# Fewer, larger loads between the two layers of a cached decode step on one core

## The chip, the cores and the metric

The kernel runs on one core of one Trainium2 chip. Its engines here are TensorE (PE, with its weight loads as PEld), VectorE (DVE), ScalarE (ACT), GpSimd (POOL) and SyncE (SP), and SP issues the transfers, which the core's 16 DMA engines carry out. The metric is the device time of one execution in microseconds (us), the median of several runs. One further execution is profiled, and every time of a stage below is from it.

## The reference

Two equal layers run over four tokens (B = 4) of width D = 512. Each layer is attention over a cache, then a gated feed-forward:

```
x = x + A(layernorm(x))      # q = x@wq (32 heads of 128); per kv head g of 8: scores q.k over 4096 positions,
                             # softmax, times v; concat @ wo
x = x + B(layernorm(x))      # silu(x@w1) * (x@w3), width 1792, then @ w2
# the same A and B, with the same cache and weights, once more
```

All is float32. Both layers read the whole K and V cache (each 4 x 8 x 4096 x 128, 64 MiB), so almost all of the time's work is the reading of some 298 MB, while the arithmetic has only 16 rows per kv head.

## The kernel before, in words

**Memory.** One large tile, `arena`, of 218 units (a unit is 256 floats, 1 KB, in each of 128 partitions, so 128 KB in all) holds everything that is loaded. Units 0 to 63 are for wq, 64 to 127 for wo, 128 to 191 for what is kept between layers (V of kv head 7, `TURN`), and units 192 to 215 are a **ring** that the feed-forward's weights pass through, together with the four units at `WO` (64 to 67). Units 214 and 215 of the ring are, until the last attention step of layer 0, part of the turned probabilities `pT`.

**Order.** The list `plan` is written at build time: every load, with the units where it goes, or none (then the first free place that is large enough is taken). `pump` issues loads from it strictly in order, all from SP, as long as the next one's units have been given back. `done` and `vacate` give units back when the work that reads them has been written, and in the running program SP waits there for that work's semaphore. So a load that has to wait holds up all later ones. Completion counters of the loads are eight in number and are taken in turn, so a load also waits until the eighth load before it has landed.

**Layer 0.** Per kv head: `scores` (PE, from K), softmax pieces on DVE and ACT, `weigh` (PE, from V). K and V of a head come as loads of 64 units (8 MB).

**Between the layers.** After the last `weigh`, the kernel runs `busy(14)` (matmuls without use that fill PE's time), `project_o` for the eight heads from wo, `collect` (the sum over heads, and the residual and norm's first part), and `feed_forward`: products with w1's and w3's first 256 columns of each quarter (`w1a`, `w3a`: four pieces each of 4 units, one per 128 rows of D), then the remaining 192 columns (`w1b`, `w3b`: four pieces of 3 units), and w2 (`down`, seven pieces of 4 units). Then `project_q` of layer 1 and the first K, whose first half comes as seven pieces called `half` through the same ring. Each product starts as soon as its piece has landed, and gives its units back when its matmuls are done. For wo, `project_o(g)` reads 8 units per head, in order of g; in the kernel before, wo comes in five loads of 32, 16, 8, 4 and 4 units, so heads 0 to 3 wait for the first alone.

**Layer 1** runs the heads in reverse order, and its last feed-forward uses larger pieces already.

The lines that the prediction speaks of: `project_o`'s matmuls (L497 for heads 0 to 6, L490 for head 7, which also is `down`), the filling matmuls of `busy` (L293) and `idle` (L299), `collect` (L336, L339), the feed-forward's products (L530), and SP's issues (L183).

Of the kernel before, what the change touches and what calls it, by code (L numbers as in the profile page):

```python
# [30 lines left out]
KB = 256  # L31
ARENA = 218
TURN = HKV - 1
SPLIT = 4
# [4 lines left out]
def tile_decode_layers(ctx: ExitStack, tc: tile.TileContext, x, kt, v, wq, wo, w1, w3, w2, w2s, out):  # L39
    nc = tc.nc  # L40
# [8 lines left out]
    WQ, WO, KEPT = 0, 64, 128  # L49
# [6 lines left out]
    def take(n, at=None):  # L56
        if at is not None and at < WO:
            return at
        for i, (lo, size) in enumerate(free):
            if at is None and state["next"] > ring["to"]:  # L60

                end = min(lo + size, PT)
                if lo < WO + 4 and end > WO:
                    if WO - lo >= n:
                        end = WO
                    else:
                        lo = WO + 4
                if end - lo < n:
                    continue
                a = lo  # L70
                lo, size = free[i]
            else:
                a = lo if at is None else at
            if lo <= a and a + n <= lo + size:
                free[i:i + 1] = [(p, s) for p, s in ((lo, a - lo), (a + n, lo + size - a - n)) if s]
                return a
        return None
# [10 lines left out]
    def load(src, per, keys, at=None):  # L88
        plan.append((src, per, keys, at))

    def cache(which, layer, g, parts, skip=0):
        src = (kt if which == "k" else v)[g]
        r = 8 * skip
        for n in parts:
            at = KEPT + r if (which, layer, g) in (("v", 0, TURN), ("k", 1, TURN - 2)) else None
            load(src[:, r * KB:(r + n) * KB], 8, [(which, layer, g, r // 8 + j) for j in range(n // 8)], at)
            r += n

    def weights(name, src, layer, parts, per, at=None, first=0):
        r = 0  # L100
        for n in parts:
            load(src[:, r * KB:(r + n) * KB], per, [(name, layer, first + r // per + j) for j in range(n // per)],
                 None if at is None else at + r)
            r += n

    order = [list(range(HKV)), list(reversed(range(HKV)))]
# [5 lines left out]
        else:  # L112
            cache("v", 0, n - 1, (64,))
    cache("v", 0, TURN, (32, 32))
    weights("wo", wo, 0, (32, 16, 8, 4, 4), 4, WO)

    def piece(name, i, at):

        w, layer, lo, n, per = {"w1a": (w1, 0, 4 * i, 4, 4), "w3a": (w3, 0, 4 * i, 4, 4),
                                "w1b": (w1, 0, 16 + 3 * i, 3, 3), "w3b": (w3, 0, 16 + 3 * i, 3, 3),  # L120
                                "w2": (w2, 0, 4 * i, 4, 2), "half": (kt[TURN], 1, 4 * i, 4, 4)}[name]
        weights(name, w[:, lo * KB:(lo + n) * KB], layer, (n,), per, at, 2 * i if name == "w2" else i)

    RING = KEPT + 64
    slots = [WO] + [RING + 4 * i for i in (5, 4, 3, 2, 1, 0)]
    for i in range(4):
        piece("w1a", i, (slots[6], slots[1], slots[2], slots[3])[i])
    for i in range(4):
        piece("w3a", i, (slots[4], slots[5], slots[0], slots[6])[i])
    for i in range(4):  # L130
        piece("w1b", i, RING + 21 - 3 * i)
    for i in range(2):
        piece("w3b", i, RING + 9 - 3 * i)
    piece("w2", 0, slots[0])
    for i in range(2, 4):
        piece("w3b", i, RING + 9 - 3 * i)
    for i in range(1, 7):
        piece("w2", i, slots[i])
    for i in range(7):
        piece("half", i + 1, slots[i])  # L140
    ring["to"] = len(plan) - 1
    cache("k", 1, TURN, (8, 8, 16), SPLIT)
    for n in range(1, HKV):
        cache("k", 1, order[1][n], {1: (8, 8, 8, 8, 16, 16), 2: (32, 32)}.get(n, (64,)))
        if n > 1:
            cache("v", 1, order[1][n - 1], (32, 32) if n == HKV - 1 else (64,))
    cache("v", 1, 0, (32, 16, 16))
# [16 lines left out]
    def pump():  # L164
        while state["next"] < len(plan):
            src, per, keys, at = plan[state["next"]]
            n = src.shape[-1] // KB
            if isinstance(per, slice):

                if keys not in where:  # L170
                    a = take(n)
                    if a is None:
                        return
                    where[keys] = a
                    nc.gpsimd.memset(arena[:, a * KB:(a + n) * KB], 0.0)
                a = where[keys]
                nc.sync.dma_start(arena[per, a * KB:(a + n) * KB], src)  # L177
                state["next"] += 1
                continue
            a = take(n, at)  # L180
            if a is None:
                return
            nc.sync.dma_start(arena[:, a * KB:(a + n) * KB], src)  # L183
            i = state["next"]
            if i == 0:
                nc.sync.dma_start(xt[:8], x[:8])
            left[i] = (len(keys), a, n)
            for j, key in enumerate(keys):
                where[key] = (a + j * per, per, i)
            state["next"] += 1  # L190
# [5 lines left out]
    def done(*key):  # L196
        i = where[key][2]
        k, a, n = left[i]
        left[i] = (k - 1, a, n)
        if k == 1:  # L200
            give(a, n)
            pump()

    def vacate(*key):
        a, n, _ = where[key]
        give(a, n)
        pump()

    xt = const.tile([P, KC, B], F32, name="xt")
    nc.scalar.dma_start(xt[8:], x[8:])  # L210
    pump()

    ident = const.tile([P, P], F32, name="ident")
    make_identity(nc, ident)
    few = const.tile([P, 4], F32, name="few")
    one, half, spare, unit = (few[:, i:i + 1] for i in range(4))
# [495 lines left out]
```

## Time and profile before

| what | before |
|---|---|
| median of 3 runs | 704.77 us (704.68 to 704.85) |
| profiled execution | 704.5 us |
| its span | 702.7 us, so 1.8 us lie around it |
| HBM read | 298.33 MB, mean 425 GB/s over the span |
| PE busy | 402.9 us (57%) |
| DVE, ACT, POOL busy | 85.2, 38.0, 7.0 us |
| loads and stores | 96 |

The span begins with the first instruction of the program and ends with the last. A PE row of the timeline gives start, length, line, output and inputs, count, and in brackets the idle time before it and what ended that. "x8" in the trace counts passes: a float32 matmul appears there twice.

### The profile page before, as it was taken

To read this page: it belongs to the slowest core of one execution; us is meant where nothing else is said; L and a number is where in the kernel's file an instruction comes from. 1 tells how busy PE (TensorE), PEld (TensorE's weight loads), DVE (VectorE), ACT (ScalarE), POOL (GpSimd) and SP (SyncE) were. 2 spreads that over 40 slices of the span, in tenths; PEclk is the share of its full clock that TensorE was granted. 3 is DMA by queue.
4 is the path that set the end of the run, shared out by engine and by line. 5 is a ranking of instruction groups with operands and counts; after the bars stand their busy time and mean duration, and the time that the engine had idled before them with its cause. 6 is when DMAs were issued, how large, how long until landed. Compare 5 with 4: busy or idle time off the path is not lost. (4 is left out here: it accounts for less than half of the span.)

```text
span 702.7 us, 7079 instructions
## 1 busy us (share of the span) xinstructions
PE 402.9 (57%) x3172; PEld 135.5 (19%) x3172; DVE 85.2 (12%) x291; ACT 38.0 (5%) x87; POOL 7.0 (1%) x12
## 2 busy tenths in 40 slices
PE   2555453555555454447888884365564545467677
PEld 1112011111111111112233321011120111122234
DVE  2001010101001010101111111020010101010111
ACT  0000000000000000102001000000000000000100
POOL 0000000000000000000000000000000000001000
PEclk9986787767778777779999997588787878788899
DMA  9999999999999999999999999999999999999997
GB/s 418 429 407 466 422 422 422 451 426 425 430 451 422 429 430 444 425 421 427 415 405 408 416 437 441 448 425 419 452 433 425 422 451 426 433 419 432 420 426 287
DMA packets 13174, 298.85 MB, mean 425 GB/s; under 512 B 1608, under 2 KB 1736, under 8 KB 6216
## 3 DMA queue, kind: packets, MB, share of 16 engines
q1 hardware_dynamic: 13008, 298.39, 99.2%
q8 instruction: 25, 0.41, 0.2%
q14 instruction: 6, 0.04, 0.0%
q10 hardware_dynamic: 135, 0.01, 0.0%
HBM read 298.33 MB, written 0.07 MB: 425 GB/s over the span
## 5 line engine op out<-in xcount | busy, mean ns | idle before, releaser
L462 PE MATMUL o_ps<-arena 128*32 128x512 f32 x1024 | 143.1, 706 | 149.6 <-DMA arena<-in_v 137.7
L415 PE MATMUL s_ps<-arena,qpad 128*32 128x512 f32 x1020 | 147.5, 732 | 92.0 <-DMA arena<-in_kt 92.0
L462 PEld LDWEIGHTS o_ps<-arena 128*32 128x32 f32 x1024 | 37.0, 127 | 253.3 <-issue 224.3
L415 PEld LDWEIGHTS s_ps<-arena,qpad 128*32 128x32 f32 x1020 | 39.3, 131 | 183.9 <-issue 176.4
L471 DVE SCALAR_TENSOR_TENSOR p<-o_ps,parts,p 128x512 f32<-128x512 f32 x16 | 12.0, 751 | 267.4 <-PE o_ps L462 267.4
L425 DVE TENSOR_REDUCE top<-s_ps 128x1 f32<-128x512 f32 x16 | 11.1, 691 | 196.6 <-PE s_ps L415 196.6
L469 ACT ACTIVATE p<-o_ps,parts 128x512 f32<-128x512 f32 x16 | 11.0, 687 | 188.5 <-PE o_ps L462 182.3
L293 PE MATMUL m_ps<-ident,rows 128*32 128x256 f32 (+1 forms) x84 | 20.9, 352 | 0.0
L353 PE MATMUL o_ps<-arena,xpad 128*32 128x512 f32 x112 | 15.5, 676 | 7.8 <-DMA arena<-in_wq 7.8
L448 PE MATMUL t_ps<-ident,p 128*128 128x128 f32 x64 | 10.9, 295 | 13.5 <-ACT p L442 13.5
L475 PE MATMUL t_ps<-ident,p 128*128 128x128 f32 x64 | 10.5, 287 | 13.9 <-DVE p L471 13.8
L435 ACT ACTIVATE f<-d 128x1 f32<-128x1 f32 x16 | 3.2, 203 | 251.0 <-DVE d L433 251.0
L497 PE MATMUL x_ps<-arena,qT 128*4 128x512 f32 x112 | 13.8, 592 | 5.1 <-DVE qT L483 3.6
L442 ACT ACTIVATE p<-s_ps,top 128x512 f32<-128x512 f32 x16 | 10.9, 684 | 75.9 <-PE t_ps L475 75.9
L449 DVE COPY arena<-t_ps 128x512 f32<-128x512 f32 x16 | 11.1, 691 | 9.3 <-PE t_ps L448 9.3
L475 PEld LDWEIGHTS t_ps<-ident,p 128*128 128x128 f32 x64 | 6.7, 140 | 28.0 <-DVE p L471 28.0
L448 PEld LDWEIGHTS t_ps<-ident,p 128*128 128x128 f32 x64 | 7.0, 145 | 22.2 <-ACT p L442 19.2
L293 PEld LDWEIGHTS m_ps<-ident,rows 128*32 128x32 f32 x84 | 9.0, 110 | 9.0 <-issue 3.5
L530 PE MATMUL s_ps<-arena,xpad 128*32 128x192 f32 (+1 forms) x128 | 7.9, 359 | 1.5 <-DMA arena<-in_w 1.5
L530 PE MATMUL o_ps<-arena,xpad 128*32 128x192 f32 (+1 forms) x128 | 8.1, 359 | 1.0 <-DMA arena<-in_w 0.9
L490 PE MATMUL x_ps<-arena,qT 128*4 128x256 f32 x88 | 6.6, 379 | 2.4 <-DMA arena<-in_w 1.7
L353 PEld LDWEIGHTS o_ps<-arena,xpad 128*32 128x32 f32 x112 | 3.5, 121 | 17.2 <-DMA arena<-in_wq 8.7
(108 smaller groups left out, 147.6 us busy)
## 6 DMA issues: line engine op xcount, KB each, us to landing
arena<-in_v SPq DMA_DIRECT2D x5, 4096.0 KB, 38.4
arena<-in_w SPq DMA_DIRECT2D x17, 512.0 KB, 9.3
arena<-in_kt SPq DMA_DIRECT2D x2, 4096.0 KB, 18.7
arena<-in_wq SPq DMA_DIRECT2D x1, 7168.0 KB
arena<-in_kt SPq DMA_DIRECT2D x6, 1024.0 KB, 11.2
arena<-in_kt SPq DMA_DIRECT2D x3, 2048.0 KB, 16.7
arena<-in_wo SPq DMA_DIRECT2D x1, 4096.0 KB, 24.0
arena<-in_v SPq DMA_DIRECT2D x2, 2048.0 KB, 36.9
```

The source lines that it names most:

```text
L293: nc.tensor.matmul(m_ps[0:32, (4 - w) * P:], rows, ident.unsqueeze(1).broadcast_to([P, w, P]), start=True, stop=True)
L353: nc.tensor.matmul(ps[32 * k:32 * k + 32, :], xpad[:, 32 * k + lo:32 * k + lo + 32], w[:, k, :], start=first, stop=last)
L415: nc.tensor.matmul(s_ps[32 * b:32 * b + 32, :], qpad[:, 32 * b + lo:32 * b + lo + 32], k[:, j, :], start=(blk == 0), stop=(blk == NB - 1))
L425: nc.vector.tensor_reduce(top[:, 0:1], s_ps, axis=AX.X, op=ALU.max, negate=True)
L448: nc.tensor.transpose(t_ps[:, i, :], p[:, i * P:(i + 1) * P], ident)
L449: nc.vector.tensor_copy(pT.rearrange("p i r -> p (i r)"), t_ps.rearrange("p i r -> p (i r)"))
L462: nc.tensor.matmul(o_ps[32 * b:32 * b + 32, :], pT[:, i, 32 * b:32 * b + 32], w[:, b, :], start=(i == 0), stop=(i == NI - 1))
L469: nc.scalar.activation(p, o_ps, AF.Copy, scale=st["parts"][:, 0:1])
L471: nc.vector.scalar_tensor_tensor(p, o_ps, st["parts"][:, 1:2], p, op0=ALU.mult, op1=ALU.add)
L475: nc.tensor.transpose(t_ps[:, j, :], p[:, j * P:(j + 1) * P], ident)
L497: nc.tensor.matmul(x_ps[r:r + B, :], left(2 * i + n), w(n), start=first, stop=False)
L530: nc.tensor.matmul(ps[32 * j:32 * j + 32, lo:lo + n], x32[:, k, :], w[:, j * n:(j + 1) * n], start=(k == 0), stop=(k == KC - 1))
```

## The change

It changes the loads only: which pieces are joined, where they go, and one queue.

- wo comes in loads of 48, 8, 4 and 4 units instead of 32, 16, 8, 4 and 4.
- w1a stays at four pieces of 4. Of w3a, pieces 0 and 1 are one load of 8. w1b and w3b come in pairs of 6. Of w2, pieces 1 and 2, and 3 and 4, are pairs of 8. The halves 2 to 7 come in three pairs of 8. The places in the ring follow from that.
- K of head 7 (its second part) is 16 + 16 instead of 8 + 8 + 16; K of head 6 is 16, 16 and 32 instead of four 8s and two 16s.
- x comes in one load from SP behind wq's first part, instead of 120 rows from ACT and 8 from SP.

That is 15 loads fewer on SP and one less on ACT, 80 in place of 96 with the store. The bytes are the same.

```diff
-    weights("wo", wo, 0, (32, 16, 8, 4, 4), 4, WO)
+    weights("wo", wo, 0, (48, 8, 4, 4), 4, WO)
...
-    slots = [WO] + [RING + 4 * i for i in (5, 4, 3, 2, 1, 0)]
+    def piece(name, i, at, n=1):
+        src, layer, lo, size, per = {"w1a": (w1, 0, 0, 4, 4), "w3a": (w3, 0, 0, 4, 4),
+                                     "w1b": (w1, 0, 16, 3, 3), "w3b": (w3, 0, 16, 3, 3),
+                                     "w2": (w2, 0, 0, 4, 2), "half": (kt[TURN], 1, 0, 4, 4)}[name]
+        lo += size * i
+        weights(name, src[:, lo * KB:(lo + size * n) * KB], layer, (size * n,), per, WO if at is None else RING + at,
+                i * size // per)
...
-    for i in range(4):
-        piece("w1a", i, (slots[6], slots[1], slots[2], slots[3])[i])
-    for i in range(4):
-        piece("w3a", i, (slots[4], slots[5], slots[0], slots[6])[i])
-    for i in range(4):
-        piece("w1b", i, RING + 21 - 3 * i)
...
+    for i in range(4):
+        piece("w1a", i, 4 * i)
+    piece("w3a", 0, 16, 2)
+    piece("w3a", 2, None)
+    piece("w3a", 3, 0)
+    piece("w1b", 0, 4, 2)
+    piece("w1b", 2, 10, 2)
+    piece("w3b", 0, 16, 2)
+    piece("w2", 0, None)
+    piece("w3b", 2, 0, 2)
+    piece("w2", 1, 6, 2)
+    piece("w2", 3, 16, 2)
+    piece("w2", 5, 0)
+    piece("w2", 6, 4)
+    piece("half", 1, None)
+    piece("half", 2, 8, 2)
+    piece("half", 4, 16, 2)
+    piece("half", 6, 0, 2)
...
-    cache("k", 1, TURN, (8, 8, 16), SPLIT)
+    cache("k", 1, TURN, (16, 16), SPLIT)
...
-        cache("k", 1, order[1][n], {1: (8, 8, 8, 8, 16, 16), 2: (32, 32)}.get(n, (64,)))
+        cache("k", 1, order[1][n], {1: (16, 16, 32), 2: (32, 32)}.get(n, (64,)))
...
-                nc.sync.dma_start(xt[:8], x[:8])
+                nc.sync.dma_start(xt, x)
...
-    nc.scalar.dma_start(xt[8:], x[8:])
```

SP's queue from wo on, in the kernel before. `arena_66` is the arena, 1024 floats are 4 units, `DMAHW0` to `DMAHW7` are the eight completion counters, and the engines' names stand for the semaphores by which SP knows that units are free:

```order
L183 DMA arena_66<-in_wo 128x8192 [waits DMAHW2_49,PE_49]
L183 DMA arena_66<-in_wo 128x4096 [waits PE_49]
L183 DMA arena_66<-in_wo 128x2048 [waits PE_49]
L183 DMA arena_66<-in_wo 128x1024 [waits PE_49] x2
L183 DMA arena_66<-in_w1 128x1024
L183 DMA arena_66<-in_w1 128x1024 [waits DMAHW3_49,DVE_49,PE_49]
L183 DMA arena_66<-in_w1 128x1024 [waits DMAHW4_49]
L183 DMA arena_66<-in_w1 128x1024 [waits DMAHW5_49]
L183 DMA arena_66<-in_w3 128x1024 [waits DMAHW6_49]
L183 DMA arena_66<-in_w3 128x1024 [waits DMAHW7_49]
L183 DMA arena_66<-in_w3 128x1024 [waits DMAHW0_49,DVE_49,PE_49]
L183 DMA arena_66<-in_w3 128x1024 [waits DMAHW2_49,DMAHW1_49,PE_49]
```

The same place of the queue with the change:

```order
L188 DMA arena_66<-in_wo 128x12288 [waits DMAHW1_49,PE_49]
L188 DMA arena_66<-in_wo 128x2048 [waits PE_49]
L188 DMA arena_66<-in_wo 128x1024 [waits PE_49] x2
L188 DMA arena_66<-in_w1 128x1024 x2
L188 DMA arena_66<-in_w1 128x1024 [waits DMAHW2_49]
L188 DMA arena_66<-in_w1 128x1024 [waits DMAHW3_49]
L188 DMA arena_66<-in_w3 128x2048 [waits DMAHW4_49,DVE_49,PE_49]
L188 DMA arena_66<-in_w3 128x1024 [waits DMAHW5_49,DVE_49,PE_49]
L188 DMA arena_66<-in_w3 128x1024 [waits DMAHW6_49,DMAHW0_49,PE_49]
```

The two first loads of wo have become one, so the matmuls of heads 0 to 5 hang on one landing. The wait for `pT`'s units (DVE) has moved from w1a's second piece to the joined w3a load, which in turn waits for wo's large load (`DMAHW4`). The last row, w3a's piece 3, goes in both kernels into the units of w1a's piece 0 and so waits for PE to have read that.

The order of instructions on PE is the same in both. These are PE's rows of the kernel before at that place, from the filling behind the last `weigh` on:

```order
L293 MATMUL m_ps<-ident,rows 32x256 x7
L497 MATMUL x_ps<-arena,qT 4x512 x16
L293 MATMUL m_ps<-ident,rows 32x256 x3
L497 MATMUL x_ps<-arena,qT 4x512 x8
L293 MATMUL m_ps<-ident,rows 32x256
L497 MATMUL x_ps<-arena,qT 4x512 x4
L293 MATMUL m_ps<-ident,rows 32x256
L490 MATMUL x_ps<-arena,qT 4x256 x4
L293 MATMUL m_ps<-ident,rows 32x256
L490 MATMUL x_ps<-arena,qT 4x256 x4
```

Sixteen matmuls are heads 0 to 3, the next eight heads 4 and 5, then head 6 and head 7's two halves. Nothing of it moved; what moved is the load that the first of them waits for.

More of the change, by code (lines that the diff above doesn't have):

```diff
@@ L114, in tile_decode_layers @@
     cache("v", 0, TURN, (32, 32))
-    weights("wo", wo, 0, (32, 16, 8, 4, 4), 4, WO)
[L117 to L122, printed above, removed]
@@ L124, in tile_decode_layers @@
-    RING = KEPT + 64
-    slots = [WO] + [RING + 4 * i for i in (5, 4, 3, 2, 1, 0)]
-    for i in range(4):
-        piece("w1a", i, (slots[6], slots[1], slots[2], slots[3])[i])
-    for i in range(4):
-        piece("w3a", i, (slots[4], slots[5], slots[0], slots[6])[i])
-    for i in range(4):
-        piece("w1b", i, RING + 21 - 3 * i)
[L132 to L140, printed above, removed]
+    weights("wo", wo, 0, (48, 8, 4, 4), 4, WO)
+    RING = KEPT + 64
+    def piece(name, i, at, n=1):
[5 more added lines that the diff above has]
+                i * size // per)
```

## The prediction

> **What bounds the kernel now.** I read the page's slices and queues first, then the busy time by stages, then the chain of waits.
>
> ```profile
> DMA  9999999999999999999999999999999999999997
> ...
> q1 hardware_dynamic: 13008, 298.39, 99.2%
> ```
>
> SP's one queue keeps the 16 DMA engines busy for 99.2% of the span. By stages (columns: stretch, length, busy time and count of PE, PEld, DVE, ACT, POOL, granted PE clock, DMA share, GB/s):
>
> ```profile
> 30.00:320.00 290.00, 147.54 (x1034) 45.04 (x1026) 30.45 (x96) 12.04 (x30) 0.61 (x1) 0.75 1.00 433
> 340.00:400.00 60.00, 53.83 (x493) 21.91 (x491) 7.97 (x33) 4.66 (x11) 1.10 (x2) 1.00 1.02 409
> 430.00:640.00 210.00, 113.65 (x754) 32.41 (x758) 22.03 (x67) 8.34 (x20) 0.00 (x0) 0.77 1.00 432
> ```
>
> Attention of both layers moves 432 to 433 GB/s. Between the layers, where the small pieces are, the engines are just as busy (share 1.02) but move 409. The chain ends on the same queue, with a tail of 3.8 us behind the last weights (702.7 - 698.9):
>
> ```profile
> 683.82 15.04 DMA arena<-in_w
> 698.86 0.04 issue
> 698.90 0.62 PE x_ps L557 x16
> ```
>
> So the time is the queue's: the cost of each load on the DMA engines, plus any moment in which an engine has nothing queued. PE matters only where it frees units too late.
>
> **Term 1: fifteen loads fewer.** The packets of that slow stretch, 340 to 400 us:
>
> ```profile
> DMA packets 5444, 24.54 MB, mean 409 GB/s; under 512 B 605, under 2 KB 605, under 8 KB 4701
> ```
>
> 5444 - 605 = 4839 row packets, 128 a load: 37.8 loads. 24.54 MB at 433 GB/s would take 56.7 us; it took 60. The 3.3 us over 37.8 loads are 0.087 us each, so 15 loads are **1.3 us**. Bounds: 1.0 (some of the 3.3 is instruction fetch, which has its own queue) to 1.6 (the 433 has some of this cost in it). x is worth nothing either way: it moves from ACT to SP in place of a load that SP issues anyway, and layer 0's first matmuls run while the first 8 MB of K are still on their way.
>
> At this point stands a rule of the Trainium skill, "DMA: Bandwidth & Descriptors", section "Anatomy of one DMA": about 2.0 us fixed per DMA, beside its bytes. By it the term would be some 30 us (an estimate: 15 x 2). The trace disagrees, since 37.8 loads with 2 us each would not fit into 60 us that also move 24.5 MB: with several loads queued the fixed part lies under the others.
>
> **Term 2: wo's first load is late, and PE with it.** PE's rows there (start, length):
>
> ```profile
> 340.13 3.21 PE L293 MATMUL m_ps<-ident,rows 128*32 128x256 f32 x14
> 344.60 3.62 PE L497 MATMUL x_ps<-arena,qT 128*4 128x512 f32 x32 [1.27 <-DMA arena<-in_wo]
> 348.04 1.46 PE L293 MATMUL m_ps<-ident,rows 128*32 128x256 f32 x6
> 349.51 1.90 PE L497 MATMUL x_ps<-arena,qT 128*4 128x512 f32 x16
> 351.23 0.59 PE L293 MATMUL m_ps<-ident,rows 128*32 128x256 f32 x2
> 352.07 1.04 PE L497 MATMUL x_ps<-arena,qT 128*4 128x512 f32 x8 [0.25 <-DMA arena<-in_wo]
> 352.93 0.59 PE L293 MATMUL m_ps<-ident,rows 128*32 128x256 f32 x2
> 353.44 0.61 PE L490 MATMUL x_ps<-arena,qT 128*4 128x256 f32 x8
> 354.62 0.62 PE L490 MATMUL x_ps<-arena,qT 128*4 128x256 f32 x8 [0.16 <-DMA arena<-in_wo]
> 355.06 0.81 PE L299 MATMUL o_ps<-ident,rows 128*32 128x384 f32 x2
> 357.40 1.71 PE L530 MATMUL s_ps<-arena,xpad 128*32 128x256 f32 x24
> ```
>
> Heads 0 to 3 start at 344.60 with the 32 units, heads 4 and 5 at 349.51 with the next 16. With 48 units in one load all six wait for about 349.4 (349.47, less 0.1 for the load saved). From 344.60 to 355.06 are 10.46 us, of which about 1.0 is waiting for wo's pieces (0.2 before 349.51, 0.4 before 352.07, 0.1 before 353.44, 0.3 before 354.62). That leaves 9.5 us of work, and none of wo's later pieces would be late any more: the end comes at 349.4 + 9.5 = **358.9** in place of 355.06. `collect` takes 355.06 to 357.40, 2.3 us, so w1a starts at 361.2 in place of 357.40.
>
> Behind the filling, PE would also stand idle from 343.34 (340.13 + 3.21) to 349.4, 6.1 us, in place of 1.3. What such a pause does, the trace shows in layer 0:
>
> ```profile
> 213.56:217.75 4.19, 0.00 (x1) 0.03 (x2) 0.00 (x0) 0.00 (x0) 0.00 (x0) 0.50 0.87 375
> 217.75:220.39 2.64, 2.64 (x16) 0.76 (x20) 0.00 (x0) 0.00 (x0) 0.00 (x0) 0.50 1.20 521
> 251.11:256.46 5.35, 0.00 (x0) 0.03 (x1) 0.00 (x0) 0.00 (x0) 0.00 (x0) 0.50 0.91 392
> 256.46:261.35 4.89, 4.89 (x24) 1.33 (x28) 0.00 (x0) 0.00 (x0) 0.00 (x0) 0.50 0.99 429
> 261.35:265.94 4.59, 4.59 (x44) 1.22 (x36) 0.00 (x0) 0.00 (x0) 0.00 (x0) 1.00 1.07 460
> ```
>
> In the pause the granted clock falls to 0.50, and it stays there for the first 2.6 to 4.9 us of work (24 matmul passes in 4.89 us, then 44 in 4.59). The stretch 340:400 above has 1.00 throughout, so today `project_o` runs warm. Cold for 2.6 to 4.9 us it loses half of that, 1.3 to 2.5; I take **2.0**, nearer the longer row, since the pause is as long as there (5.35). w1a then starts at 363.2.
>
> The Trainium skill ("TensorE: Matmul & The Clock Gate", "Part 1: The HAM clock gate") states the same and its cause: a free-running window of about 3.4 us, one idle window halves the clock and one busy window restores it. By its figure the loss would be at least 1.7 us (an estimate, half of 3.4), which would make term 2 worth 0.3 less than by my rows.
>
> **Term 3: when the queue runs dry.** The ring holds 24 + 4 units. w3a's piece 3 goes, in both kernels, where w1a's piece 0 was, so SP issues it when PE has read that:
>
> ```profile
> 358.10 0.33 SPq L183 DMA_DIRECT2D arena<-in_w  x1
> ...
> 363.59 0.64 PE L530 MATMUL o_ps<-arena,xpad 128*32 128x256 f32 x8 [0.23 <-DMA arena<-in_w]
> 364.87 0.64 PE L530 MATMUL o_ps<-arena,xpad 128*32 128x256 f32 x8 [0.23 <-DMA arena<-in_w]
> ```
>
> It went out at 358.10, 0.70 us after w1a began, and landed at 364.8; the load ahead of it landed at 363.55. So the queue had 5.4 us left at the issue. With the change the load ahead lands at 363.4, while the issue comes at 363.2 + 0.7 = 363.9. How soon do bytes follow an issue into an empty queue? The last store shows it:
>
> ```profile
> 700.34 0.35 SPq L671 DMA_DIRECT2D out<-p  x1
> ...
> 700.70:701.10 0.40, 0.00 (x0) 0.00 (x0) 0.00 (x0) 0.00 (x0) 0.00 (x0) 1.00 0.00 0
> 701.10:701.30 0.20, 0.00 (x0) 0.00 (x0) 0.00 (x0) 0.00 (x0) 0.00 (x0) 1.00 0.37 118
> ```
>
> 0.9 us. So all engines start again at 364.8, **1.4 us** after the last of them ran dry. Bounds: 0 (PE stays warm: issue 361.9, bytes 362.8, before 363.4) and 1.9 (2.5 lost).
>
> That is the last engine. The others were ahead, and lose their lead:
>
> ```profile
> 694.00:695.00 1.00, 1.00 (x37) 0.96 (x34) 0.18 (x1) 0.00 (x0) 0.00 (x0) 1.00 0.98 373
> 695.00:696.00 1.00, 0.49 (x6) 0.01 (x1) 0.00 (x0) 0.00 (x0) 0.00 (x0) 1.00 0.75 299
> 697.00:698.00 1.00, 1.00 (x34) 0.71 (x26) 0.00 (x0) 0.00 (x0) 0.00 (x0) 1.00 0.57 229
> 698.00:699.00 1.00, 0.38 (x16) 0.10 (x8) 0.00 (x0) 0.00 (x0) 0.00 (x0) 1.00 0.42 145
> ```
>
> At the end of the stream the 16 engines finish between 694.3 and 698.9. A lead that some had at 363 may be what pays for their later extra work: the four w2s loads of layer 1 have four rows of 16 KB each, so at most four engines carry them, 4 x 0.6 = 2.4 us there (an estimate, 16 KB at 432/16 GB/s). If those engines start level with the last one at 364.8, they end later than it. Bounds: 0 (the engines with extra work are those that lag already) and 2.4. I take **1.3**, about the middle, as no view names the engines.
>
> After this stall the later refills keep up: w1b's first pair goes out when w1a's piece 2 is read, 1.1 us after the load that stalled, and the stalled load moves for 1.3 us (364.87 - 363.59). Downstream, K of layer 1 in 16s and 32 instead of 8s is free: PE reaches K's later blocks with several us of queue in front, and the order on PE doesn't move.
>
> **Sum.** -1.3 + 1.4 + 1.3 = +1.4 us. The profiled execution is 704.5 (span 702.7 and 1.8 around it), so 705.9 for one like it, and the median of the runs lies 0.27 above it: **706.2**.
>
> **The rivals.**
> - *PE is late but warm.* 3.8 us late, the engines ahead run dry and the last doesn't: -1.3, plus part of the lead, about 0.9: 704.4. For it: the last engine's margin is 363.4 - 362.8 = 0.6. Against: every pause of over 4 us in the rows above turned the clock down.
> - *Nothing stalls.* Leads suffice, or PE gets its work done sooner: 704.77 - 1.3 = 703.5, at best 703.2. For it: 5.4 us of queue ahead of the issue today. Against: the 9.5 us of `project_o` are all work, and 3.8 of them can't be hidden.
> - *The refill stays behind PE (slower).* With all engines level no one has a lead, and w3b's first pair and second pair go out only about 0.8 us before the queue ends (w3a's joined load must be read before the former, and it is PE that comes 5.9 us late). Each time PE misses by 1 us the queue stops for it; with one more such stop of 1 to 2 us it is 707.8. It decides from 0.8 us of further delay on PE.
> - *The fixed cost of each load was exposed*: the store above takes 1.6 us from issue to landing, 15 of those are 24 us, 681. The rate of 409 GB/s rules it out but for 1 in 100.
>
> **How the numbers follow.** Forecast (stall of all engines) 0.50, late but warm 0.19, nothing stalls 0.18, refill behind PE 0.12, exposed cost 0.01. A change of 0.2%, 1.4 us, is about what a measurement of this kernel can tell from none. The forecast's own range is 705.0 to 707.6, and six tenths of it lie above 706.2: slower 0.30 + 0.12 with some of the rest, 0.44. Same: 0.20 of the forecast, 0.17 of warm, 0.08 of no stall, 0.45. Faster: half of no stall and the exposed cost, 0.11. Range for 8 in 10: 703.4 (no stall at the best rate, nearly) to 708.0.
>
> **What would show it.** Right: PE's first L497 of layer 0 near 349.4, behind wo; granted clock below 1 between 344 and 355; w1a's L530 near 363; DMA share below 1 between 361 and 365, and nowhere else before the end; a rate of some 420 GB/s from 366 to 400. Term 1 is wrong if that rate stays at 409. Term 2 is wrong if the clock stays 1.00 or w1a starts before 361. Term 3 is wrong if the share stays at 1 with w1a that late; its lead part is wrong if the time after 365 isn't lengthened against before.

## The result, and the profile after

The changed kernel takes **712.39 us** (median, 711.84 to 713.82) against 704.81 us for the kernel before (704.68 to 705.01): ratio 1.011, interval 1.0093 to 1.0128. It is 7.6 us slower, where 1.4 slower was forecast; the range ended at 708.0. The profiled execution took 712.6, with a span of 710.8.

The page of the changed kernel, slices and queue:

```profile
DMA  9999999999999999999979999999999999999996
...
q1 hardware_dynamic: 10976, 298.40, 98.1%
```

One slice has a 7 where all were 9, and the queue's share went from 99.2% of 702.7 us to 98.1% of 710.8. Both are 697 us (697.1 and 697.3; the packets' own times add to 696.8 and 697.6): they took about as long in sum as before, and most of the 8 us are time in which engines had no packet. The equal sums hide a saving and a loss, which stand under term 1 below. The same stretches of both kernels show how much (columns as in the prediction: stretch, length, busy time and count of PE, PEld, DVE, ACT, POOL, PE clock, DMA share, GB/s). Before:

```profile
340.00:360.00 20.00, 18.09 (x148) 6.77 (x146) 2.70 (x9) 0.47 (x2) 0.00 (x0) 1.00 1.00 409
360.00:370.00 10.00, 8.37 (x94) 3.83 (x86) 1.46 (x6) 0.89 (x2) 0.55 (x1) 1.00 1.03 403
370.00:400.00 30.00, 27.37 (x260) 11.32 (x259) 3.81 (x18) 3.29 (x7) 0.55 (x1) 1.00 1.02 411
400.00:430.00 30.00, 19.43 (x168) 6.18 (x168) 7.36 (x24) 2.43 (x7) 0.00 (x0) 0.98 1.03 435
```

With the change:

```profile
340.00:360.00 20.00, 13.89 (x82) 4.35 (x83) 1.75 (x4) 0.00 (x0) 0.00 (x0) 0.83 0.98 404
360.00:370.00 10.00, 9.72 (x109) 5.52 (x108) 1.91 (x10) 0.95 (x3) 0.55 (x1) 1.00 0.55 195
370.00:400.00 30.00, 25.01 (x269) 11.91 (x265) 3.78 (x17) 3.34 (x7) 0.55 (x1) 1.00 0.99 390
400.00:430.00 30.00, 24.12 (x185) 7.50 (x178) 4.45 (x14) 1.93 (x5) 0.00 (x0) 0.83 1.01 428
430.00:640.00 210.00, 112.76 (x768) 32.48 (x765) 25.44 (x79) 9.21 (x23) 0.00 (x0) 0.77 1.00 432
```

The bytes that are missing in a stretch, at 432 GB/s, are its price: (409 - 404) x 20 us = 0.1 MB or 0.2 us; (403 - 195) x 10 = 2.08 MB or **4.8 us**; (411 - 390) x 30 = 0.63 MB or **1.5 us**; (435 - 428) x 30 = 0.21 MB or 0.5 us. Together 7.0 of the 8.1 us by which the span grew. From 430 to 640 both kernels move 432. The other 1.1 are lost at the very end, in the last five us of the weights, first before and then with the change:

```profile
694.00:699.00 5.00, 3.49 (x92) 2.39 (x92) 0.18 (x1) 0.00 (x0) 0.00 (x0) 1.00 0.69 268
```

```profile
702.00:707.00 5.00, 3.73 (x89) 2.50 (x88) 0.18 (x1) 0.00 (x0) 0.00 (x0) 1.00 0.47 180
```

The share falls by 0.22, 1.1 us: the 16 engines finish further apart. That this comes from the stall isn't shown. By the single packets the mean engine is without work for 1.9 us from 640 to the last weights before and for 3.1 with the change, but also for 2.9 in a kernel that has no stall and the median time of before (the one with only the joins with slack, below).

The stretches from 340 to 430 hold two kinds of loss, which the finer stretches of the changed kernel tell apart:

```profile
360.00:362.00 2.00, 2.00 (x22) 0.90 (x21) 0.00 (x0) 0.00 (x0) 0.00 (x0) 1.00 0.53 217
362.00:363.00 1.00, 1.00 (x7) 0.38 (x5) 0.43 (x2) 0.40 (x2) 0.00 (x0) 1.00 0.17 70
363.00:364.00 1.00, 1.00 (x10) 0.97 (x10) 0.16 (x1) 0.07 (x1) 0.00 (x0) 1.00 0.02 8
364.00:365.00 1.00, 1.00 (x18) 0.55 (x22) 0.35 (x2) 0.00 (x0) 0.00 (x0) 1.00 0.00 0
365.00:366.00 1.00, 1.00 (x25) 0.55 (x18) 0.00 (x0) 0.00 (x0) 0.00 (x0) 1.00 0.33 41
...
365.00:370.00 5.00, 4.72 (x66) 2.73 (x59) 0.98 (x5) 0.47 (x1) 0.55 (x1) 1.00 0.85 288
...
390.00:400.00 10.00, 10.00 (x90) 3.74 (x92) 1.42 (x8) 0.96 (x2) 0.55 (x1) 1.00 1.00 397
```

In the kernel before the last of these stretches read:

```profile
390.00:400.00 10.00, 9.88 (x90) 3.51 (x89) 0.67 (x3) 0.37 (x1) 0.00 (x0) 1.00 1.01 420
```

From 360 on one engine after the other runs out of work: the queue is dry. By the single packets of this trace the last engine ends at 363.21, and the next packet begins at 365.89.

From 390 to 400 the share is almost that of before, 1.00 and 1.01, and yet 397 GB/s move in place of 420. The single packets show where the rest went. Call the median duration of a size in a trace its usual one, and a packet long that takes over 1.5 times that. Of the 357 row packets (2 KB and more) that begin here 14 are long (up to 2.0 us), and what they took beyond the usual is 0.4 us of the ten, as a mean over the 16 engines. Before, 4 of 384 are long, for 0.1 us. The usual 8 KB packet is not slower: 0.309 us, and 0.312 before. So the share counts an engine as busy while it is held by one packet. The same is seen right behind the dry stretch, where the first 19 packets of 4 KB take 0.19 to 0.92 us in place of 0.16. From 370 to 400 as a whole the share falls by 0.03, 0.9 us, and the rate by 1.5 us, so both kinds are in it.

PE's rows, which answer to those from 340.13 to 357.40 in the prediction (the lines are now L297 for the filling, L501 for `project_o`, L303 for `idle`, L534 for the feed-forward's products, L494 for head 7 and `down`):

```profile
340.52 3.21 PE L297 MATMUL m_ps<-ident,rows 128*32 128x256 f32 x14
349.84 6.20 PE L501 MATMUL x_ps<-arena,qT 128*4 128x512 f32 x32 [6.11 <-DMA arena<-in_wo]
...
361.90 0.81 PE L303 MATMUL o_ps<-ident,rows 128*32 128x384 f32 x2
...
364.23 1.50 PE L534 MATMUL s_ps<-arena,xpad 128*32 128x256 f32 x24
...
373.91 0.53 PE L534 MATMUL s_ps<-arena,xpad 128*32 128x192 f32 x8 [1.69 <-DMA arena<-in_w]
...
378.94 0.53 PE L534 MATMUL o_ps<-arena,xpad 128*32 128x192 f32 x8 [0.97 <-DMA arena<-in_w]
...
381.43 0.61 PE L494 MATMUL x_ps<-arena,qT 128*4 128x256 f32 x8 [1.21 <-DMA arena<-in_w]
```

PE waits 6.11 us for wo's large load, takes 6.20 us for the 32 passes that took 3.62, and reaches w1a at 364.23 in place of 357.40. After that it waits for loads again and again. The load of w3a's piece 3, on SP's queue, follows PE as before by 0.70 us (358.10 then):

```profile
364.93 0.33 SPq L188 DMA_DIRECT2D arena<-in_w  x1
```

The end of the chain of waits is the same as before, 8.1 us later (the last weights landed at 698.86):

```profile
691.66 15.33 DMA arena<-in_w
706.98 0.04 issue
707.02 0.62 PE x_ps L561 x16
```

### The profile page after: what moved, and what is told of

It is laid out like the page before. It is cut to its first block, busy times and chain, and to the rows that moved or that the text cites. A ratio compares the mean times of both kernels' runs of the same rounds, so it can differ in the third digit from the quotient of the medians.

```text
span 710.8 us, 7048 instructions
## 1 busy us (share of the span) xinstructions
PE 408.7 (57%) x3172; PEld 138.0 (19%) x3172; DVE 85.1 (12%) x291; ACT 38.0 (5%) x87; POOL 7.0 (1%) x12
## 3 DMA queue, kind: packets, MB, share of 16 engines
q1 hardware_dynamic: 10976, 298.40, 98.1%
## 5 line engine op out<-in xcount | busy, mean ns | idle before, releaser
L466 PE MATMUL o_ps<-arena 128*32 128x512 f32 x1024 | 145.5, 717 | 149.8 <-DMA arena<-in_v 138.1
L419 PE MATMUL s_ps<-arena,qpad 128*32 128x512 f32 x1020 | 149.7, 742 | 89.2 <-DMA arena<-in_kt 89.2
L501 PE MATMUL x_ps<-arena,qT 128*4 128x512 f32 x112 | 17.1, 693 | 9.7 <-DMA arena<-in_wo 6.1
L297 PE MATMUL m_ps<-ident,rows 128*32 128x256 f32 (+1 forms) x84 | 20.9, 352 | 0.0
L297 PEld LDWEIGHTS m_ps<-ident,rows 128*32 128x32 f32 x84 | 9.0, 110 | 9.3 <-issue 3.6
L534 PE MATMUL o_ps<-arena,xpad 128*32 128x192 f32 (+1 forms) x128 | 8.8, 359 | 1.5 <-DMA arena<-in_w 1.5
L534 PE MATMUL s_ps<-arena,xpad 128*32 128x192 f32 (+1 forms) x128 | 8.3, 357 | 2.1 <-DMA arena<-in_w 2.1
L494 PE MATMUL x_ps<-arena,qT 128*4 128x256 f32 x88 | 7.7, 379 | 2.3 <-DMA arena<-in_w 1.8
```

What stands on the lines that cost most here:

```text
L297: nc.tensor.matmul(m_ps[0:32, (4 - w) * P:], rows, ident.unsqueeze(1).broadcast_to([P, w, P]), start=True, stop=True)
L419: nc.tensor.matmul(s_ps[32 * b:32 * b + 32, :], qpad[:, 32 * b + lo:32 * b + lo + 32], k[:, j, :], start=(blk == 0), stop=(blk == NB - 1))
L466: nc.tensor.matmul(o_ps[32 * b:32 * b + 32, :], pT[:, i, 32 * b:32 * b + 32], w[:, b, :], start=(i == 0), stop=(i == NI - 1))
L501: nc.tensor.matmul(x_ps[r:r + B, :], left(2 * i + n), w(n), start=first, stop=False)
L534: nc.tensor.matmul(ps[32 * j:32 * j + 32, lo:lo + n], x32[:, k, :], w[:, j * n:(j + 1) * n], start=(k == 0), stop=(k == KC - 1))
```

## The experiments

Two theories stood against each other at the start: that wo's large load does it all, by stalling the queue once (then splitting it again should give back the whole), or that the joined loads cost something by themselves. Each kernel below is timed against the kernel before on the same chip; 704.7 to 704.9 is its median throughout.

### wo split again

```diff
-    weights("wo", wo, 0, (48, 8, 4, 4), 4, WO)      # the changed kernel
+    weights("wo", wo, 0, (32, 16, 8, 4, 4), 4, WO)
```

> The changed kernel with wo in 32, 16, 8, 4 and 4 units again, all other joined loads kept (81 loads and stores). Theory A (the stall comes from wo's large load: PE starts project_o 5 us late and at half clock): project_o starts near 345 with clock 1.00, the DMA share stays at 1 from 360 to 370, and the time falls from 712.4 to 703.8, 1.0 below the kernel before (14 loads fewer at 0.087 us, less some for x behind wq). Rival B (the joined pieces in the ring come free too late, whatever PE does before): it stays above 709.

Measured 708.23 us (706.59 to 709.19), ratio 1.0041 (1.0028 to 1.0054): by the medians 4.2 less than the changed kernel, still 3.5 more than before. That is neither theory's number, but it is near the second's: the joined loads cost something by themselves. The stretches of this kernel:

```profile
370.00:375.00 5.00, 3.79 (x53) 2.19 (x52) 0.52 (x2) 1.91 (x3) 0.00 (x0) 1.00 1.02 352
375.00:380.00 5.00, 3.04 (x28) 1.26 (x27) 0.42 (x1) 0.00 (x0) 0.00 (x0) 0.73 0.89 334
380.00:385.00 5.00, 4.71 (x47) 1.84 (x38) 0.62 (x3) 0.00 (x0) 0.00 (x0) 0.93 0.96 334
```

The kernel before, over the same 15 us:

```profile
370.00:385.00 15.00, 12.49 (x132) 5.73 (x135) 2.05 (x9) 1.96 (x4) 0.00 (x0) 1.00 1.03 408
```

The dry stretch around 364 is gone, but from 370 to 385 the queue moves 334 to 352 GB/s in place of 408. In the last two rows the share is below 1, in the first it is not. There 22 of 253 row packets are long and took 0.8 of the 5 us beyond the usual, where none of 543 is long before. The profiled execution took 709.19, the longest of the five.

### wo joined alone

```diff
-    weights("wo", wo, 0, (32, 16, 8, 4, 4), 4, WO)  # the kernel before
+    weights("wo", wo, 0, (48, 8, 4, 4), 4, WO)
```

> The kernel before with wo in 48, 8, 4 and 4 units, nothing else changed. Theory A: PE is late as in the changed kernel (w1a starts near 364, clock 0.50 before), the small pieces stall behind it just the same: 711 to 714. Rival B: the small pieces come free one by one, so the queue recovers: 704.8 to 706.

Measured 709.49 us (708.73 to 710.04), ratio 1.0065 (1.0049 to 1.008): 4.8 us for this load alone, between the two theories.

```profile
360.00:365.00 5.00, 5.00 (x56) 2.84 (x49) 0.93 (x5) 0.47 (x2) 0.00 (x0) 1.00 0.35 105
365.00:370.00 5.00, 4.72 (x57) 2.88 (x60) 1.46 (x6) 0.47 (x1) 0.55 (x1) 1.00 0.97 376
370.00:375.00 5.00, 3.45 (x53) 2.12 (x52) 0.52 (x2) 1.91 (x3) 0.00 (x0) 1.00 1.02 401
```

The same dry stretch as in the changed kernel, but with all other pieces small the rate is back at 401 right behind it. Against 403 before, the two first rows miss (298 + 27) x 5 us = 1.6 MB, 3.8 of the 4.8 us. That is the first kind of loss, and it is one stall.

### The pause filled

How much of that is the cold clock, and how much the lateness? The pause is filled with idle matmuls, which compute nothing that is used, first in the changed kernel and then in the one with wo's load alone.

```diff
-            busy(14)
+            busy(41)
```

> The changed kernel with the filling before project_o lengthened from 14 to 41 units (matmuls without use, about 5.8 us), so that PE stands still for some 0.5 us before wo lands. Theory A: the clock stays 1.00, project_o takes 9.5 us in place of 12.1, w1a starts near 361.5 in place of 364.2, the queue is empty for at most 3 us on the engines ahead and not at all on the last: 705 to 708. If the clock is no part of it: w1a still near 364, 712.

> The kernel before with wo's large load of 48 units, all other pieces small, and the pause of PE filled with 41 idle matmuls in place of 14 (they compute nothing that is used), so that it stays warm; project_o is as late as before, but not slow. Theory: filling took 2.1 us off the changed kernel, and takes 2 off the 709.49 that wo's load gives alone: 707.0 to 708.0, share between 0.5 and 0.8 in 360 to 365. Rival (with small pieces lateness alone is absorbed, the cold clock decides): 704.7 to 706.0, share near 1 in 360 to 365.

Measured 710.28 us (708.86 to 712.26), ratio 1.0075 (1.0059 to 1.0092), for the changed kernel so filled, 2.1 less than without, and more than the 705 to 708 expected. Its PE rows:

```profile
349.61 3.62 PE L501 MATMUL x_ps<-arena,qT 128*4 128x512 f32 x32
...
361.40 1.50 PE L534 MATMUL s_ps<-arena,xpad 128*32 128x256 f32 x24
```

The 32 passes take 3.62 us again, and w1a starts at 361.40, 2.8 earlier. Yet most engines still run out of work: the share from 360 to 365 is 0.57. The filled kernel with wo's load alone measured 708.49 us (707.41 to 709.39), ratio 1.0052 (1.0039 to 1.0065), 1.0 less than unfilled, and neither theory's number (707.0 to 708.0, or 704.7 to 706.0):

```profile
360.00:365.00 5.00, 4.72 (x51) 3.05 (x50) 1.01 (x8) 0.47 (x2) 0.00 (x0) 1.00 0.67 229
365.00:370.00 5.00, 4.87 (x62) 2.69 (x61) 1.13 (x3) 0.47 (x1) 0.55 (x1) 1.00 0.89 311
```

So a warm PE that is merely late already costs 3.7 us (2.7 to 4.6 by the interval). By the medians the cold clock adds 1.0 to 2.1; the 1.0 is not clear of the noise of its two kernels. The rival that the cold decides is out.

### x in one load, and K joined

```diff
-                nc.sync.dma_start(xt[:8], x[:8])        # the kernel before, x
+                nc.sync.dma_start(xt, x)
-    nc.scalar.dma_start(xt[8:], x[8:])
...
-    cache("k", 1, TURN, (8, 8, 16), SPLIT)              # the kernel before, K
+    cache("k", 1, TURN, (16, 16), SPLIT)
-        cache("k", 1, order[1][n], {1: (8, 8, 8, 8, 16, 16), 2: (32, 32)}.get(n, (64,)))
+        cache("k", 1, order[1][n], {1: (16, 16, 32), 2: (32, 32)}.get(n, (64,)))
```

> The kernel before with x in one load of 128 rows from SP, none from ACT. In the changed kernel the first K packets start 0.1 to 0.3 us later than before. If x's 64-byte rows in the one queue are the cause, the time rises by 0.1 to 0.4 us, to 704.9 to 705.2; if they are free, as the prediction had it, 704.8.

> The kernel before with K of layer 1 alone in the changed kernel's sizes (head 7: 16 and 16, head 6: 16, 16 and 32), 92 loads and stores. Theory A (a joined load goes out later, because it needs all its units, and what counts is how long before the engines reach it): head 7's first 16 go out at 387.1 in place of 385.7, when the engines ahead finish the halves at 387.6; they stop for 0.5 to 1 us, the others don't: 704.6 to 705.5. If K's joins are free as the prediction had it: 4 x 0.087 less, 704.4.

x: 705.0 us (704.76 to 705.99), ratio 1.0003 (0.9994 to 1.0012), which can't be told from no change. K: 705.5 us (705.16 to 705.93), ratio 1.0008 (0.9999 to 1.0017), 0.6 more. K's joins take four loads away and save at best 0.1 us by the interval; the forecast's price of 0.087 us a load would have saved 0.35.

### The pairs of the feed-forward

With wo split again, first all of w2 and the halves in single pieces; then, in addition, K and x as before, which leaves the pairs of w3a, w1b and w3b alone, at their new places in the ring:

```diff
-    piece("w2", 1, 6, 2)
-    piece("w2", 3, 16, 2)
-    piece("w2", 5, 0)
-    piece("w2", 6, 4)
-    piece("half", 1, None)
-    piece("half", 2, 8, 2)
-    piece("half", 4, 16, 2)
-    piece("half", 6, 0, 2)
+    for i, at in enumerate((6, 10, 16, 20, 0, 4)):
+        piece("w2", i + 1, at)
+    for i, at in enumerate((None, 8, 12, 16, 20, 0, 4)):
+        piece("half", i + 1, at)
```

> The changed kernel with wo in five loads (708.2 as measured) and in addition w2 and the halves in single pieces of 4 units; w3a's, w1b's and w3b's pairs stay (86 loads and stores). Theory A with w2's and the halves' joined pieces as the place: the rate from 370 to 390 comes back from about 340 to 400 GB/s: 704.2 to 705.5. Rival: the pairs of w1b, w3a and w3b have already used up the engines' lead: 707 to 708.5.

> Only the pairs of w3a, w1b and w3b are joined (with w2 and the halves in single pieces at the places this leaves them); wo, K and x are as before. Theory: the kernel with wo split and w2 and halves single stands at 707.29, and K's joins and x were worth 0.6 and 0.2 to 0.3 by themselves, so the pairs alone give 706.3 to 706.6, with a rate under 390 GB/s somewhere in 360 to 380. Rival: the pairs cost only together with the other joins (a level queue): 704.6 to 705.4 and about 405 GB/s throughout.

Measured 707.29 us (706.07 to 709.91), ratio 1.0035 (1.0021 to 1.0048), as the rival had it, and for the pairs alone 706.33 us (705.68 to 707.28), ratio 1.0021 (1.0013 to 1.003), as the theory had it. Five loads fewer, no stall at wo, a warm clock, and 1.5 us slower. The pairs alone:

```profile
365.00:370.00 5.00, 3.53 (x52) 2.04 (x45) 0.48 (x1) 0.15 (x1) 0.00 (x0) 1.00 0.99 384
370.00:375.00 5.00, 3.76 (x56) 2.10 (x60) 0.61 (x3) 1.76 (x3) 0.00 (x0) 1.00 0.99 374
375.00:380.00 5.00, 4.24 (x46) 1.62 (x45) 0.51 (x2) 0.00 (x0) 0.00 (x0) 1.00 1.00 374
```

The kernel before, over the same 15 us:

```profile
365.00:380.00 15.00, 11.82 (x141) 5.28 (x141) 1.60 (x5) 1.91 (x3) 0.00 (x0) 1.00 1.03 405
```

The share falls by 3 or 4 hundredths, half a us in 15, and the rate from 405 to some 377, (405 - 377) x 15 us = 0.42 MB or 1.0 us. Of 1210 row packets 33 are long and took 1.0 us beyond the usual; before, 5 of 1653 and 0.1 us. At no time are all engines without work here. A pair gives its units back only when both of its pieces have been read, so a load into them is issued later, when less is queued in front of it. How much less can be estimated from the traces: the bytes of the loads issued before, less those of the packets that have begun, at 432 GB/s. For the weight loads issued between 358 and 376 that is 2.2 to 3.5 us with the pairs, and 2.9 to 4.4 in the kernel before. No run separates the pairs from the places that they take.

### One number: where w2's first pair lies

In the changed kernel w2's pieces 1 and 2 lie at units 6 to 13 of the ring and piece 6 at 4 to 7, so piece 6 can't be issued until PE has read the pair's first piece. Two units further on it doesn't touch it. wo is split again here too.

```diff
-    piece("w2", 1, 6, 2)
+    piece("w2", 1, 8, 2)
```

> The changed kernel with wo in five loads, and w2's pieces 1 and 2 at units 8 to 15 of the ring in place of 6 to 13, so that w2's piece 6 (units 4 to 7) no longer waits for them but for w3b alone; the number of loads is the same (81). Theory A: w2's piece 6 goes out right behind piece 5, some 2.5 us earlier: 705.5 to 707. Rival (the size of the pieces alone counts, not where they lie): 708.2.

Measured 706.37 us (705.79 to 708.31), ratio 1.0022 (1.0013 to 1.003): 1.9 us less than with the pair at 6. With the pair at 6, SP's last two loads of w2 and the matmul in between read so (pieces 5 and 6):

```profile
374.95 0.33 SPq L188 DMA_DIRECT2D arena<-in_w  x1
...
377.96 0.33 SPq L188 DMA_DIRECT2D arena<-in_w  x1
```

```profile
377.09 0.86 PE L494 MATMUL x_ps<-arena,qT 128*4 128x256 f32 x8 [1.97 <-DMA arena<-in_w]
```

Piece 6 went out 3.0 us behind piece 5, when PE had read what landed at 377.09. With the pair at 8 both went out together:

```profile
374.80 0.81 SPq L188 DMA_DIRECT2D arena<-in_w  x2
```

The rate there answers:

```profile
375.00:380.00 5.00, 3.04 (x31) 1.19 (x31) 0.28 (x1) 0.00 (x0) 0.00 (x0) 1.00 0.97 386
380.00:385.00 5.00, 4.71 (x48) 2.71 (x48) 0.98 (x6) 0.47 (x2) 0.00 (x0) 1.00 1.03 417
```

It is 386 and 417 in place of 334 and 334. By the estimate of the last section, piece 6 had 3.4 us of queue in front of it, and 1.1 with the pair at 6. Nothing but one place in memory differs, so this loss came from when a load could be issued, not from its size. How large it is remains rough: the profiled execution with the pair at 8 took 705.79 us and the one with the pair at 6 709.19, so the rows differ by more than the medians.

### Only the joins with slack; all joins of the ring

Two kernels ask whether any part is worth keeping. The first is the kernel before with the halves in three pairs and K of head 6 in 16, 16 and 32, that is six loads fewer:

```diff
-    for i in range(7):
-        piece("half", i + 1, slots[i])
+    piece("half", 1, slots[0])
+    for i in (2, 4, 6):
+        weights("half", kt[TURN][:, 4 * i * KB:(4 * i + 8) * KB], 1, (8,), 4, RING + 24 - 4 * i, i)
...
-        cache("k", 1, order[1][n], {1: (8, 8, 8, 8, 16, 16), 2: (32, 32)}.get(n, (64,)))
+        cache("k", 1, order[1][n], {1: (16, 16, 32), 2: (32, 32)}.get(n, (64,)))
```

> The kernel before with the halves 2 to 7 in three pairs and K of head 6 in 16, 16 and 32, all else as before (90 loads and stores). Each joined load there has over 3 us of queue ahead of it by the trace of before. Theory A: nothing goes late, 6 x 0.087 us less: 704.2. Rival (every joined load in the ring costs): above 705.

Measured 704.85 us (704.24 to 706.54), ratio 1.0000 (0.9991 to 1.0009). A gain of 0.5 us (six loads at 0.087) is neither shown nor excluded.

The second is the kernel of the section above (wo split, w2's pair at 8) with K and x as before:

> All joins of the ring are kept, with w2's first pair two units further on; wo, K of heads 7 and 6 and x are as before. Theory (costs add): 706.37 less 0.6 (K) and 0.2 to 0.3 (x), 705.4 to 705.7. Rival (K's joins cost nothing behind a ring that has already lost its lead): 706.1 to 706.4.

Measured 707.23 us (705.5 to 707.35), ratio 1.0031 (1.002 to 1.0042). That is 0.9 more than with K joined and x in one, where 0.7 to 1.0 less was expected from adding the costs, and the rival's 706.1 to 706.4 is missed too. Its runs fall into two groups, two at 705.5 to 705.8 and five at 707.1 to 707.4, and the profile shows one of the lower group, so what makes the upper one isn't known. By its median the adding of costs was off by 1.5 to 1.8 us, so single prices here are good to between 1 and 2 us and no better, and which of two kernels that differ by less is the faster isn't settled.

No kernel that was run beats the kernel before.

### What the 7.6 us are made of

| part | how measured | us |
|---|---|---|
| wo's load of 48 units | alone, 709.49 | +4.8 |
| of it without the cold clock | alone and filled, 708.49 | +3.7 |
| pairs of w3a, w1b, w3b | alone, 706.33 | +1.5 |
| w2 and halves in pairs, at these places | wo split again (+3.5) less the same with them single (+2.4) | +1.1 |
| K | alone, 705.5 | +0.6 |
| x | alone, 705.0 | +0.3 |

Each is the difference of medians to the kernel before in the same series. The parts add to 8.3 in place of 7.6; those of K and x can't be told from nothing, and that the sum comes so near is partly luck, by the last experiment.

## Why the prediction was wrong

Its bottleneck, its place and its sign were right: PE's first product waits for wo, the clock falls, PE reaches w1a late, and the queue runs dry between 361 and 365. The size was wrong, 7.6 in place of 1.4. Two steps failed: the sentences that put the joined loads behind the stall at nothing, where they cost 3.5 us without any stall, and the price of the dry queue, 4.8 in place of 2.7. The 1.1 us at the end of the stream stand in no term.

**Term 1, -1.3 (fewer loads): there in the packets, not shown in the time.** It took all of the 3.3 us by which 340 to 400 is slower than attention for a cost of loads, and divided. The packets bear its price out. Before, the usual row of 3 KB takes 0.124 us, of 4 KB 0.162 and of 8 KB 0.312; with the change, the usual row of 6 KB takes 0.234. So joining two rows saves 0.012 to 0.014 us, and joining two loads (128 rows on 16 engines) about 0.1 us (an estimate from these durations), where 0.087 was taken. With every row at its usual duration, taken over all traces of this study, the packets of the changed kernel take 1.2 us less than those before. What they took beyond that grew from 3.1 to 5.1 us. In the time no run shows the saving: five loads fewer gave +1.5 and four gave +0.6; six gave 0.0 with an interval of 0.6 to either side. The sign that the prediction named, a rate of some 420 behind the stall, came out at 390, but as late refills lower the rate too, this says nothing of the term. The 2.0 us that the prediction quotes there from the Trainium skill ("DMA: Bandwidth & Descriptors", "Anatomy of one DMA") are that section's fit for transfers issued by GpSimd; here SyncE issues them.

**Term 2, w1a at 363.2: 364.23, right in kind and 1.0 too small.** The first product started at 349.84, not 349.4. The clock:

```profile
343.73:349.84 6.11, 0.00 (x0) 0.00 (x1) 0.00 (x0) 0.00 (x0) 0.00 (x0) 0.87 0.90 381
349.84:355.10 5.26, 5.26 (x28) 1.00 (x32) 1.29 (x2) 0.00 (x0) 0.00 (x0) 0.50 1.02 405
```

It was 0.50 for all of the first 5.26 us of work, and heads 0 to 3 lost 6.20 - 3.62 = 2.6 where 2.0 was taken and 2.5 was the upper bound. The Trainium skill ("TensorE: Matmul & The Clock Gate", "Part 1: The HAM clock gate") gives about 3.4 us of window, by which the loss is at least 1.7 (an estimate, half of it). This trace agrees with that as a lower bound; the rows of layer 0 were the nearer guide. With wo joined alone the pause is the same 6.11 us, and the cold was shorter:

```profile
349.59 5.07 PE L497 MATMUL x_ps<-arena,qT 128*4 128x512 f32 x32 [6.11 <-DMA arena<-in_wo]
```

Its stretch at half clock:

```profile
349.59:352.56 2.97, 2.97 (x16) 0.56 (x20) 1.29 (x2) 0.00 (x0) 0.00 (x0) 0.50 1.02 408
```

There the loss was 5.07 - 3.62 = 1.45 us, so that trace lies below the estimate of 1.7. So the same pause cost 1.45 us in one profiled execution and 2.6 in another, and how far the 2.0 was off is partly chance. The rest was right: from 361.90, where `project_o` ended, to w1a are 2.33 us of `collect`, and the 9.5 us of work are 361.40 - 2.33 - 349.61 = 9.46 in the changed kernel with the pause filled.

**Term 3, the dry queue: +2.7 forecast (1.4 stall and 1.3 lead), 4.8 measured.** The last engine ran dry at 363.21, as forecast (363.4). The issue came at 364.93 in place of 363.9, and the first packet 0.96 behind it, at 365.89, so the stall of the last engine was 2.7 in place of 1.4. The other engines ran out from 360.0 on, and by 363.21 had lost 1.9 us as a mean over all 16, in place of the 1.3 that was taken as the middle of 0 to 2.4. These two make 4.6 of the 4.8. The lead was a real loss, and 1.0 of the 1.3 us by which the stall was longer is the delay of PE that term 2 had too small.

**"After this stall the later refills keep up" and "K of layer 1 is free": the step that failed outright.** From 370 to 430 the change lost another 2.0 us, with PE waiting 0.97 to 1.69 us at three pieces, and without any stall at wo the joined pieces cost 3.5 (wo split again). The prediction checked whether a refill still comes *before* the queue ends. It did in most places. What it didn't see is that a pair makes every refill behind it later, and that a refill which comes shortly before the end also costs: with 1.1 us of queue in front of w2's last piece in place of 3.4, the kernel was 1.9 us longer. K alone measured +0.6, which can't be told from nothing.

**The rivals.** "The refill stays behind PE", 707.8, held 0.12 and was the nearest: it expects later refills to stop the queue again, but comes to 3.0 of the 7.6 us. "Late but warm" is out by the clock, and the filled kernels show that it would not have given 704.4: late and warm is 3.7 us slower by itself, with all other pieces small. "Nothing stalls" is out too, and wo split again shows that its 703.5 wasn't to be had without the stall either. The range ended at 708.0: it held one more stop of 1 to 2 us, where the joined pieces without the stall cost 3.5, and a dry queue of 2.7, where 4.8 was measured.

## What to carry to other kernels

Where small pieces go through a ring, a joined load saves about 0.1 us of the engines' time (here, by the packets), while it holds its units until its last reader and makes the consumer wait for its last byte. So estimate, for each load behind it, how much of the queue is still in front of it when it is issued, with the mean engine: the 5.4 us that the prediction counts are those of the last engine, while the mean by the bytes that had not begun was 2.9 (an estimate). Here most loads of the kernel before had 3.7 us or more, and one load with 1.1 in place of 3.4 cost 1.9 us. Leave the pieces small where few are left. Price a queue that runs dry with the mean engine, since the lead of the others is lost too. A place in the ring that touches a second piece by two units is a wait like any other; look for it in the issue times, one by one.

## What the runs showed of the hardware

- **A share of 1 is not the full rate.** With wo split again the engines showed a share of 1.02 from 370 to 375 and moved 352 GB/s; the kernel before, 1.02 to 1.03 at 403 to 411. With pairs alone it was 0.99 to 1.00 at 374 to 384. A few packets make the difference (22 of 253 from 370 to 375), each recorded for up to 2.1 us where 0.16 to 0.31 is usual. They were seen where loads go out shortly before the engines reach them and right behind a dry queue; that a late issue causes them is argued, and what an engine does in them isn't shown.
- **What a row costs.** The usual packet of 3 KB took 0.124 us, of 4 KB 0.162 and of 8 KB 0.312 in the kernel before, so joining two loads saves about 0.1 us of the 16 engines' time (an estimate from these).
- **The 16 engines of the core are not level.** They ran out of the same work from 360.0 to 363.2 in mid-kernel (share 0.53 from 360 to 362, 0.02 from 363 to 364); the forecast had seen that only at the end of the stream.
- **The clock after a pause of 6.11 us** stayed at 0.50 for the first 5.26 us of work in the changed kernel and for 2.97 with wo joined alone, where layer 0 showed 2.6 to 4.9 us after pauses of 4.2 and 5.4.
- **Times scatter more in some kernels.** The kernel before lay within 1.6 us in all series (704.45 to 706.02), the one with w2 and the halves single within 3.8, and one kernel had two separate times 1.6 us apart. Part of it is the end of the stream: the profiled execution with only the joins with slack took 705.65 in place of 704.5 before, 1.15 more, and its mean engine was without work 1.1 us longer from 640 on. The rest isn't known.
